# Two quads' pooled result repeated by matrix products instead of by a store and loads, with quad 0's mixing ordered sooner

## The chip, the cores and the metric

The kernel runs on one core of a Trainium2 chip. That core has a matrix engine (TensorE), a vector engine (VectorE), a scalar engine (ScalarE), a general engine (GpSimd) and a queue engine (SyncE) that here issues nearly all DMA transfers. Each of them works through its own list of instructions in order and meets the others by semaphores. TensorE's clock is granted at one of two levels, 1.2 and 2.4 GHz; the profile gives it as a share of the upper one.

The metric is the device time of one execution in microseconds, the median of several runs.

## The reference

The input is an attention problem of 4 batches, 8 heads, 576 rows and 64 columns, followed by two mixing networks. What matters here is the attention and the first step behind it:

```python
q_d = q.reshape(B, H, Sd, 4, D).mean(axis=3)        # likewise k_d, v_d: Sd = 144
out_d = sm_attn(q_d, k_d, v_d)                       # softmax attention on 144 rows
out_up = np.repeat(out_d, 4, axis=2)                 # each row four times: 576 rows
scores = where(abs(i - j) < 4, scale * q @ k.T, -1e9)
out_local = softmax(scores) @ v
x = (out_up + out_local)                             # heads side by side: 576 x 512
h = relu(x.T @ w_tok1) @ w_tok2                      # token mixing, 576 -> 256 -> 576
u = x + h.T
```

A channel network and a second mixing with sines and cosines follow. All is computed to float32 accuracy; where products run in the faster rounded format, each operand is split in a high and a low part and three products are added.

## The kernel before

Two heads make a pair (16 pairs, numbered 0 to 15), two pairs make a quad (8 quads, 0 to 7). For each pair, `pair_local` computes the banded attention of 576 rows in five blocks of 128 rows. For each quad, `quad_front` (L425) computes the pooled attention: scores `sd` on TensorE, row maxima `mxd` on VectorE, exponentials `pd` on ScalarE, transposes `pdt`, their copy `pts`, the product `od`, and the division on VectorE that gives `ods`. `ods` holds 144 pooled rows of four heads, and every row is needed four times, on four neighbouring partitions.

That repetition is done through memory (L509 to L519): `ods` is stored in two parts into `od_d` and `ot_d`, and read back into the tile `xu` by three loads whose source has a repeated axis. `add_pooled` (L595) then adds `xu` to the pair's local result `x`, and `token_mix` (L598) splits the sum into `xh` and `xl` and multiplies with the token weights `w1h` and `w1l`. Those weights come in as 64-bit floats and are converted in steps on ScalarE (L199, L201), VectorE (L203, L206, L215), GpSimd (L219), ScalarE (L221) and VectorE (L223).

Every such routine is a generator, cut by `yield` into steps. The table `ORDER` says in which sequence the steps are run, and thereby the order on every engine: no scheduler moves them in this part. `P` is the load of a pair's q and k, `W` of its values, `K` pools a pair, `F` is the quad's attention, `L` the pair's local attention, `A` adds the pooled result, `T` is the token mixing, `G` converts token weights. `F0` at its eighth place stores `ods` of quad 0, at its ninth it loads `xu`.

PSUM has eight banks in this part: four single ones, tag "mm", for `od` and the mixing's products, and two tiles of two banks, tag "big", through which all of `s`, `sd`, `pt`, `pdt` and `o` pass. So a product into a big tile waits until the last reader of the tile before the one before is done.

`warm` (L312) issues products on zeros ahead of the first pairs' scores. `low2` is a pool of tiles that the mixing of odd blocks uses later.

Of the kernel before, what the change touches and what calls it, by code (L numbers as in the profile page):

```python
# [12 lines left out]
F32 = mybir.dt.float32  # L13
# [17 lines left out]
FIRST = 1  # L31
ROWS = ((8, 9), (0, 2), (4, 6), (2, 3))
ORDER = """
G3 P0 G2 I*2 P1 G3 P4 G3 V0 P2 G3 K0 G3 G2 I G2 I L0*2 P3 K1 F0 W1 L0 F0 L1 L0 G3 F0 V0 L1*2 P5 V0 L2 W0 G2 K2 V0 G2
F0 G1 L1 V1 F0 L2 K3 G0 G6 K4 L0 F0 L0 L2 L1 G2 F1 L2 K5 L1 L0 F1 G1*2 F1 F0 V1 W3 L0 F1 G5 G0 L1 F0 G0 F1 G6 F2 L1 G0
P6 W2 G5 G6 L3 V1 F2 F0 V1 L3 G6 F2 F1 L3 G1 G4 F1 L2 P7 L5 L2 K6 L5 F1 G1 L3 A0 V2 X0 A1 L3 G1 T0 L5 G0 T0 L2 G2 F1
L3 G0 G4 F2 G5 T0*2 V2 X2 L2 G6 W5 F2 K7 V2 L4*2 E0.0*2 T0 L4 V3 V2 A2 L3 E0.1 L5 G4 L4 W4 L5 G6 L5 G4 L3 X2 F3 G5 P8
P9 A3 G4 F2 G5 E0.1 T1 G4 G5 T0 F2 V3 L4 F3 F2 T0 L4 V3 X2 F3 L6 V3 L6 X7 T0 P11 L6 X2 X0 F3 K8 U0.0 L6 T0 X2 X0 U0.0
F3 L4 U0.0 V4 K9 F2 F3 X0 L6 L4 L6 T1 F4 U0.1 X0 F3 T1 L5 U0.1 X0 T1 U0.1 F4 X7 X4 V4 F3 T1 X7 F4 W6 L5 X7 E1.1 F4
E1.0 E1.1 L8 V4 L8 X7 E1.0 X1 A4 F4 T1 P10 A5 T1 X2 T2 L8 T1 U1.0*2 T2 T1 U1.0 X1 F3 L7 X7 L7 T2 X1 T2 X4 X5 K10 X1 L8  # L40
L6 U1.1*2 L7 T2 E2.0 U1.1 W7 X4 L7 V4 X1 L7 F4 W9 L7 L6 X4 E2.1 E2.0 C0 E2.1 T2 X1 L8 K11 X5 L7 T2 X5 L8 W8 L9*2 L7 X5
P13 T2 P12 L9 L10 C0 A6 F5 X4 C0 U2.0 L10 U2.0 X5 U2.0 C0 X3 F5 X6 F4 F5 C0 A7 F4 L10 T3 X4 F5 L9 V5 T3 H0.1 L8 U2.1
F5 T2 H0.1 H0.0 K12 T3 L9 U2.1 X5 C0 L9 U2.1 K13 F4 X6*2 L10 T3 X3 W13 H0.0 X6 H0.2 F6 E3.0*2 V5 P14 T3 F6 V5 H0.2 F6
C0 V6 V5 L8 X3 E3.1 L9 H0.3 F5 E3.1 X3 W10 L9 F6 X3 F5 L10 V6 A9 T3 F5 T3 V6 U3.0 L10 K14 T3 V6 U3.0 X6 U3.0 T3 H0.3
# [42 lines left out]
PAIRS = ((0, 1), (5, 4))  # L87
LOWER, WIDE = 2, 2
MIX = 384
NMIX = 6  # L90
WARM = [24] + [12] * 3 + [0] * 12
DEEP = [4, 4]
# [4 lines left out]
DTOK = 256  # L97
DCH = 1536
NB = 5
# [15 lines left out]
def kernel(  # L115
# [16 lines left out]
    act, dve, pool, pe, sp = nc.scalar, nc.vector, nc.gpsimd, nc.tensor, nc.sync  # L132
# [13 lines left out]
    idt, diag, msk = fixed[:, 0:128], fixed[:, 128:132], fixed[:, 132:].bitcast(BF16)  # L146
# [19 lines left out]
    def converted(stage, hi, lo, parts, sub, add, gaps=repeat(1), room=None, keep=(), fine=0):  # L166
# [10 lines left out]
        else:  # L177
            both = room
            if isinstance(room, tuple):
                both = room[0].tile([128, 4, MIX], F32, tag=room[1], name=f"raw_{at}")  # L180
            both = both.rearrange("p k n -> p (k n)")
# [71 lines left out]
    low2 = tc.alloc_tile_pool(name="low2", bufs=1, side="right")  # L253
# [12 lines left out]
    def evict_hidden(ps, n, at):  # L266

        h1 = hp.tile([128, MIX], F32R, tag="h1", name=f"g1_{at}")
        h2 = hp.tile([128, MIX], F32R, tag="h2", name=f"g2_{at}")

# [10 lines left out]
    def columns(t, i):  # L281

        return t[:, i * MIX : i * MIX + MIX].rearrange("(k p) n -> p k n", p=128)

    mmp = ctx.enter_context(tc.tile_pool(name="mma", bufs=8 - 2 * WIDE, space=PSUM))

    actx = ExitStack()
    sb1 = actx.enter_context(tc.tile_pool(name="a1", bufs=1))
# [29 lines left out]
    loaded, values, pooled, xs_of, xus, hiddens, outs = {}, {}, {}, {}, {}, {}, {}  # L318

    def step(name, gen):  # L320
        gens[name] = gen

    def constants():
        sp.dma_start(fixed, consts)
        yield
        pool.memset(zero, 0.0)
        for t in pbuf:
            pool.memset(t, 0.0)
        yield
        act.copy(id16, idt)  # L330
        yield

    def tok1(kb, room):
# [91 lines left out]
    def quad_front(Q):  # L425
        b, hh = divmod(Q, 2)
        at = f"{b}_{hh}"
# [3 lines left out]
        for p in range(2):  # L431
            for c in range(4):
                for j in range(2):
# [4 lines left out]
                        start=True,  # L438
                        stop=True,
                    )  # L440
            for j in range(2):
                c = 2 * j + p
# [4 lines left out]
                    start=True,  # L447
                    stop=True,
# [4 lines left out]
            out=mx[:, 0:4].rearrange("p (j a) -> p j a", j=2),  # L453
# [4 lines left out]
        for j in range(2):  # L458
            r = slice(64 * j, 64 * j + 64)
# [11 lines left out]
        for j in range(2):  # L471
            r = slice(64 * j, 64 * j + 64)
# [6 lines left out]
        for o, i in ((128, 0), (256, 4)):  # L479
            for c in range(4):  # L480
                out = pt[32 * c : 32 * c + 32, 1, o : o + 128]
# [24 lines left out]
        ods = sb1.tile([128, 5, 64], F32, tag="ods", name=f"ods_{at}")  # L506
        dve.tensor_tensor(out=ods, in0=odv[:, :, 0:64], in1=rd.to_broadcast([128, 5, 64]), op=ALU.mult)
        yield
        base, tail = od_d[b][hh], ot_d[b][hh]  # L509
        sp.dma_start(base.rearrange("s k n -> k s n"), ods[:, 0:4, :].rearrange("p c d -> p (c d)"))  # L510
        sp.dma_start(tail.rearrange("s (c d) -> c s d", c=4), ods[:, 4, :])
        yield
        xu = sb1.tile([128, NB, DTOK], F32, tag="xu", name=f"xu_{b}_{hh}")
# [152 lines left out]
    def mix(i, p0, p1):  # L666
# [3 lines left out]
        if not p0:  # L670
            ut = (low2 if odd else b2).tile([128, 4, MIX], F32, tag="ut", name=f"ut_{at}")
            sp.dma_start(ut, columns(uT_d, i))
            mixes["ut", i, p0] = ut
        uh, ul = ((low2 if odd else b1).tile([128, 4, MIX], F32R, tag=f"u{p}", name=f"u{p}_{at}") for p in "hl")
        if p0:
# [233 lines left out]
    def mix_rest(i):  # L909
        ut = (cells["utx"] if i in [q for _, q in PAIRS] else b2).tile([128, 4, MIX], F32, tag="ut", name=f"ut_{i}_{LOWER}")  # L910
        sp.dma_start(ut, columns(xT_d, i))
        mixes["ut", i, LOWER] = ut
        yield
# [35 lines left out]
    def lazily(f):  # L949
        yield from f()  # L950
# [123 lines left out]
    def first_split():  # L1074
        cells["xhl0"], steps = split_x(0, cells["x0"][0])
        for st in steps:
            st()
            yield

    step("I", constants())  # L1080
    for n in range(4 * B):
        for name, f in (("P", load_pair), ("W", load_values), ("K", pool_pair), ("L", pair_local), ("A", add_pooled)):
            step(f"{name}{n}", f(n))
    for Q in range(2 * B):
        for name, f in (("V", pool_values), ("F", quad_front), ("T", token_mix)):
            step(f"{name}{Q}", f(Q))
        for i in range(2):
            step(f"E{Q}.{i}", token_hidden(Q, i))
            step(f"U{Q}.{i}", token_out(Q, i))
# [9 lines left out]
    for i in chain(range(4 * LOWER, 28), range(31 + FIRST, 39), range(41, 45)):  # L1099
        step(f"X{i}", lazily(lambda i=i: cells["X", i]()))  # L1100
    for i in range(NMIX):
        step(f"J{i}", mix_rest(i))
# [28 lines left out]
    with tc.manual_schedule(engines={act.engine, dve.engine, pool.engine, pe.engine, nc.sync.engine}):  # L1131
        for e in ORDER:
            name, _, times = e.partition("*")
# [7 lines left out]
    sb1 = ctx.enter_context(tc.tile_pool(name="c1p", reuse_waits="tile", bufs=1))  # L1141
# [75 lines left out]
    T0, T1 = slice(0, HALF), slice(HALF, S)  # L1217
# [119 lines left out]
    for b in range(B):  # L1337
        x, xn = xx
        uh = sb1.tile([128, 4, S], F32R, tag="uh", name=f"cuh_{b}")
        ul = sb1.tile([128, 4, S], F32R, tag="ul", name=f"cul_{b}")  # L1340
# [94 lines left out]
```

## Time and profile before

| | |
|---|---|
| Median of 3 runs | 685.61 us (683.41 to 687.0) |
| The profiled execution | 681.57 us, its span 679.8 us, mean granted clock 0.99 |
| TensorE busy | 655.9 us, 96% of the span |
| VectorE busy | 521.0 us, 77% |
| ScalarE busy | 321.2 us, 47% |
| GpSimd busy | 98.5 us, 14% |
| DMA | 109.93 MB, mean 162 GB/s |
| Chain that ended last | TensorE 84%, VectorE 8%, DMA 3%, ScalarE 3% |

The page's slices of 17 us show TensorE at 6, 7, 6 and 9 tenths at first and at 9 or more from then on. The DMA engines are at 7 to 8 tenths in the first slices. The attention part lies in the first 190 us, mixed with the first mixing products; the rows below are from it but for one. In a timeline row, the bracket at the end gives how long the engine stood still ahead of the row and what released it. "Issue" there means that nothing in the profile explains the idle time.

### The profile page before, as it was taken

How to read it: one execution, taken by the hardware profiler on the slowest of the kernel's cores; microseconds unless marked ns; L12 is line 12 of the kernel's file. 1: busy time of each engine (PE TensorE's matmuls, PEld its weight loads, DVE VectorE, ACT ScalarE, POOL GpSimd, SP SyncE). 2: the span in 40 equal slices, each digit the busy share in tenths (PEclk: the TensorE clock that was granted, in tenths of full speed). 3: DMA queues.
4: the chain of work that ended last, by engine and by line, in shares of the span. 5: the costliest groups of instructions: out<-in, count | busy, mean ns of one | idle time of the engine just before them, and what ended most of it. 6: DMA issues, size and time to landing. Idle time of an engine off the chain costs nothing.

```text
span 679.8 us, 17390 instructions
## 1 busy us (share of the span) xinstructions
PE 655.9 (96%) x7320; PEld 626.7 (92%) x7320; DVE 521.0 (77%) x952; ACT 321.2 (47%) x632; POOL 98.5 (14%) x92
## 2 busy tenths in 40 slices
PE   6769899999999999999999999999999999999997
PEld 4558789889999999999999999999999998998997
DVE  5889998697542888998988867677898748857837
ACT  4566667455341674535434523154647326527311
POOL 3223322305000333300101200012000000000000
PEclk9889999999999999999999999999999999999999
DMA  8787788757343785527263762699410330140202
GB/s 282 239 277 229 250 274 260 252 179 238 110 157 104 242 293 186 202 62 207 66 194 127 209 142 85 238 324 279 130 63 0 112 114 1 62 141 1 71 1 69
DMA packets 93022, 109.93 MB, mean 162 GB/s; under 512 B 46881, under 2 KB 69537, under 8 KB 92945
## 3 DMA queue, kind: packets, MB, share of 16 engines
q1 hardware_dynamic: 92080, 106.08, 49.6%
q0 software_dynamic: 864, 2.75, 1.0%
q8 instruction: 57, 0.93, 0.6%
q14 instruction: 21, 0.16, 0.1%
HBM read 79.13 MB, written 29.69 MB: 160 GB/s over the span
## 4 chain that ended last, share of the span: by engine, by line
PE 84%; DVE 8%; DMA 3%; ACT 3%; SPq 1%; issue 1%; DVEq 0%; ACTq 0%
PE y L157 6%; PE y L158 6%; PE y L159 6%; PE c L157 4%; PE c L158 4%; PE c L159 4%; PE c L699 4%; PE c L702 4%; PE c L700 4%; PE c_p L905 3%; PE c_p L902 3%; PE c_p L903 3%; PE t L157 2%; PE t L159 2%; PE t L158 2%; DMA qk<-qkT 2%
## 5 line engine op out<-in xcount | busy, mean ns | idle before, releaser
L157 PE MATMUL y<-wrh,zh 128*128 128x288 f32 x256 | 75.0, 296 | 0.8 <-ACT zh L151 0.8
L158 PE MATMUL y<-wrl,zh 128*128 128x288 f32 x256 | 74.9, 296 | 0.0
L159 PE MATMUL y<-wrh,zl 128*128 128x288 f32 x256 | 72.9, 295 | 0.0
L219 POOL TENSOR_TENSOR ww<-ww,raw 128x512 int32<-128x512 int32 (+2 forms) x30 | 41.1, 1373 | 159.2 <-DMA raw<-w_ch 52.5
L157 PEld LDWEIGHTS y<-wrh,zh 128*128 128x128 f32 x256 | 48.0, 188 | 1.1 <-ACT zh L151 1.1
L158 PEld LDWEIGHTS y<-wrl,zh 128*128 128x128 f32 x256 | 48.0, 188 | 0.0
L159 PEld LDWEIGHTS y<-wrh,zl 128*128 128x128 f32 x256 | 47.3, 188 | 0.0
L219 POOL TENSOR_TENSOR raw<-raw 128x512 int32<-128x512 int32 (+2 forms) x16 | 20.0, 1249 | 136.7 <-DVE raw L215 74.1
L1212 DVE TENSOR_TENSOR cx<-y,cx 128x288 f32<-128x288 f32 x32 | 14.4, 455 | 30.3 <-PE y L159 29.9
L151 ACT CAST cuh<-cx 128x288 fp32r<-128x288 f32 (+1 forms) x16 | 8.8, 553 | 57.5 <-DVE cx L1212 57.4
L157 PE MATMUL th<-thh,cxh 128*128 128x512 f32 (+1 forms) x92 | 31.6, 343 | 0.0
L158 PE MATMUL th<-thl,cxh 128*128 128x512 f32 (+1 forms) x92 | 31.6, 343 | 0.0
L159 PE MATMUL th<-thh,cxl 128*128 128x512 f32 (+1 forms) x92 | 31.6, 343 | 0.0
L199 ACT ACTIVATE ww<-raw 128x512 f32<-128x512 f32 (+2 forms) x30 | 19.5, 649 | 25.3 <-DVE c1l L223 9.4
L921 DVE SCALAR_TENSOR_TENSOR g<-c,g 128x384 fp32r<-128x384 f32 x40 | 21.1, 550 | 12.9 <-ACT g L918 12.9
L918 ACT ACTIVATE g<-c 128x384 fp32r<-128x384 f32 x40 | 19.1, 490 | 24.4 <-PE c L159 24.3
L201 ACT ACTIVATE raw<-raw 128x512 int32<-128x512 uint32 (+3 forms) x46 | 29.5, 640 | 0.0
L568 PE MATMUL o<-vw,plt 38*32 38x65 f32 x1280 | 18.0, 236 | 6.9 <-issue 3.6
L929 DVE TENSOR_TENSOR ut<-c,ut 128x384 f32<-128x384 f32 x32 | 17.1, 551 | 9.8 <-PE c L702 9.8
L568 PEld LDWEIGHTS o<-vw,plt 38*32 38x32 f32 x1280 | 15.4, 110 | 9.6 <-issue 4.8
L157 PE MATMUL t<-w2h,h 128*128 128x256 f32 (+1 forms) x64 | 21.6, 337 | 0.0
L157 PE MATMUL c<-uh,c1h 128*128 128x384 f32 x64 | 21.4, 334 | 0.0
(390 smaller groups left out, 2266.6 us busy)
## 6 DMA issues: line engine op xcount, KB each, us to landing
raw<-w_ch SPq DMA_DIRECT2D x27, 512.0 KB
qk<-qkT SPq DMA_DIRECT2D x16, 582.0 KB
xT<-ut SPq DMA_DIRECT2D x12, 768.0 KB
vd<-vtok SPq DMA_DIRECT2D x8, 650.0 KB
vw<-vloc SPq DMA_DIRECT2D x32, 146.2 KB
uT<-us SPq DMA_DIRECT2D x16, 288.0 KB
ut<-uT SPq DMA_DIRECT2D x6, 768.0 KB
ut<-xT SPq DMA_DIRECT2D x6, 768.0 KB
```

Of the source, the lines that this page charges most:

```text
L157: pe.matmul(out, lh, rh, start=start, stop=False, skip_group_check=again)
L158: pe.matmul(out, lh, rl, start=False, stop=False, skip_group_check=again)
L159: pe.matmul(out, ll, rh, start=False, stop=stop, skip_group_check=again)
L201: act.activation(f, words[:, :, 0], AF.Copy, scale=2.0**-29)
L219: pool.tensor_tensor(out=w.bitcast(I32), in0=w.bitcast(I32), in1=f, op=ALU.add)
L568: pe.matmul(o[r : r + 32, 5 * j + i // 2], pts[h : h + W, i // 2, r : r + 32], vw[h : h + W, g, :], start=True, stop=True,)
L699: pe.matmul(ps[:, 0:MIX], h[:, cb % 2, d], h1, start=cb == cbs[0], stop=False)
L700: pe.matmul(ps[:, 0:MIX], l[:, cb % 2, d], h1, start=False, stop=False)
L702: pe.matmul(ps[:, 0:MIX], weight[cb // 2][2][:, cb % 2, d], h2, start=False, stop=cb == cbs[-1])
L902: pe.matmul(ps[:, 0:MIX], h[:, cb % 2, d], h1, start=cb == cbs[0], stop=False)
L903: pe.matmul(ps[:, 0:MIX], l[:, cb % 2, d], h1, start=False, stop=False)
L921: dve.scalar_tensor_tensor(out=h2, in0=ps, scalar=0.0, in1=h1.bitcast(F32), op0=ALU.max, op1=ALU.subtract)
```

## The change

For quads 0 and 1 (`UP`), `quad_front` no longer stores and loads. Instead TensorE multiplies `ods` with a matrix of ones and zeros, `spread`, that has each row's one in four columns. Four products with 64 rows of contraction and 256 columns give the first 128 pooled rows, four with 128 rows and 64 columns the last 16. They go into three single PSUM banks (`up`), and ScalarE copies these into `xu`. The matrix is made once from the identity by four copies on ScalarE. The other six quads keep the store and loads.

The table is written anew in its first lines: the adds `A0` and `A1` stand ahead of pair 6's pooling, the first step of `T0` ahead of the copies of quad 1, and the load `W0` ahead of `P5`. Later lines hold the same steps.

```diff
-G3 P0 G2 I*2 P1 G3 P4 G3 V0 P2 G3 K0 G3 G2 I G2 I L0*2 P3 K1 F0 W1 L0 F0 L1 L0 G3 F0 V0 L1*2 P5 V0 L2 W0 G2 K2 V0 G2
+G3 P0 G2 I*2 P1 G3 P4 G3 V0 P2 G3 K0 G3 G2 I G2 I L0*2 P3 K1 F0 W1 L0 F0 L1 L0 G3 F0 V0 L1*2 W0 P5 V0 L2 G2 K2 V0 G2
...
+UP = (0, 1)
...
         act.copy(id16, idt)
+        both = low2.tile([128, 4, MIX], F32, tag="ul", name="spread").rearrange("p k n -> p (k n)")
+        spread["main"] = both[:, 0:256].rearrange("p (e n) -> p e n", e=2)
+        spread["rest"] = both[:, 256:768].rearrange("p (c n) -> p c n", c=4)
+        for h in range(2):
+            r = slice(64 * h, 64 * h + 64)
+            out = both[r, 0:256].rearrange("p (q r) -> p q r", r=4)
+            act.copy(out, idt[r, 64 * h : 64 * h + 64].unsqueeze(2).to_broadcast([64, 64, 4]))
+        rest = both[:, 256:768].rearrange("p (c j q r) -> p c j q r", c=4, j=2, r=4)
+        one = idt.rearrange("p (c q) -> p c q", c=4)[:, :, 16:32]
+        for j in range(2):
+            act.copy(rest[:, :, j], one.unsqueeze(3).to_broadcast([128, 4, 16, 4]))
         yield
...
+        if Q in UP:
+            xu = xus[Q] = sb1.tile([128, NB, DTOK], F32, tag="xu", name=f"xu_{b}_{hh}")
+            up = [mmp.tile([128, 512], F32, tag="mm", name=f"up_{at}_{h}") for h in range(3)]
+            for e in range(2):
+                for h in range(2):
+                    r = slice(64 * h, 64 * h + 64)
+                    out = up[h][:, DTOK * e : DTOK * e + DTOK]
+                    rhs = ods[r, 0:4, :].rearrange("p h d -> p (h d)")
+                    pe.matmul(out, spread["main"][r, e], rhs, start=True, stop=True)
+            for c in range(4):
+                out = up[2][:, 64 * c : 64 * c + 64]
+                pe.matmul(out, spread["rest"][:, c], ods[:, 4, :], start=True, stop=True)
+            yield
+            for h in range(2):
+                act.copy(xu[:, 2 * h : 2 * h + 2].rearrange("p b n -> p (b n)"), up[h])
+            act.copy(xu[:, 4], up[2][:, 0:DTOK])
+            yield
+            return
         base, tail = od_d[b][hh], ot_d[b][hh]
         sp.dma_start(base.rearrange("s k n -> k s n"), ods[:, 0:4, :].rearrange("p c d -> p (c d)"))
```

What the change moves is seen best in the order of the instructions. In these rows tiles carry batch and place in it, then a serial number: `od_0` and `xu_0` belong to quad 0, `pts_1` to quad 1, `mxd_0_728` and `pd_0_780` to quad 2, which is quad 0 of batch 1. Lines are those of each version.

TensorE at the place of the first new products, before (`o_1` is pair 1's local product):

```order
L477 MATMUL pdt_1_602<-fixed,pd_1_579 128x128 x5
L482 MATMUL pdt_1_602<-fixed,pd_1_579 32x128 x8
L568 MATMUL o_1_620<-vw_1_266,plt_1_525 32x65 x40
L434 MATMUL sd_0_672<-qkd_0_448 32x144 x8
L443 MATMUL sd_0_672<-qkd_0_448 32x144 x2
```

and with the change:

```order
L491 MATMUL pdt_1_607<-fixed,pd_1_584 128x128 x5
L496 MATMUL pdt_1_607<-fixed,pd_1_584 32x128 x8
L600 MATMUL o_1_625<-vw_1_271,plt_1_530 32x65 x40
L531 MATMUL up_0_0_667<-ods_0_594,spread 128x256
L531 MATMUL up_0_1_668<-ods_0_594,spread 128x256
L531 MATMUL up_0_0_667<-ods_0_594,spread 128x256
L531 MATMUL up_0_1_668<-ods_0_594,spread 128x256
L534 MATMUL up_0_2_669<-ods_0_594,spread 128x64 x4
L448 MATMUL sd_0_690<-qkd_0_453 32x144 x8
```

Eight products stand between pair 1's local product and quad 2's scores. Quad 1's eight follow pair 5's scores in the same way.

ScalarE at the same place, before (`raw_446` and `ww_669` are the third token weight in conversion):

```order
L199 ACTIVATE raw_444<-raw_444 128x512
L201 ACTIVATE raw_444<-raw_444 128x512
L485 COPY pts_1_666<-pdt_1_602 128x512
L486 COPY pts_1_666<-pdt_1_602 128x384
L199 ACTIVATE ww_669<-raw_446 128x288
L201 ACTIVATE raw_446<-raw_446 128x288
```

and with the change, where the same weight is `raw_451` and `ww_687`:

```order
L200 ACTIVATE raw_449<-raw_449 128x512
L202 ACTIVATE raw_449<-raw_449 128x512
L537 COPY xu_0_666<-up_0_0_667 128x512
L537 COPY xu_0_666<-up_0_1_668 128x512
L538 COPY xu_0_666<-up_0_2_669 128x256
L499 COPY pts_1_684<-pdt_1_607 128x512
L500 COPY pts_1_684<-pdt_1_607 128x384
L200 ACTIVATE ww_687<-raw_451 128x288
```

Three copies that read `up` stand ahead of quad 1's `pts` and of that weight.

ScalarE some ten rows on, before (`plt_2` is pair 2's transposed weights, `pbuf_120` pair 3's exponentials, `xh_0` quad 0's first mixing operand):

```order
L562 COPY plt_2_838<-pt_2_827 128x128
L221 CAST w1h<-raw_393 128x512
L553 ACTIVATE pbuf_120<-pbuf_120 128x10x38
L603 CAST xh_0_902<-x_0_600 128x1280
L221 CAST w1h<-raw_444 128x512
```

and with the change:

```order
L594 COPY plt_2_854<-pt_2_843 128x128
L585 ACTIVATE pbuf_120<-pbuf_120 128x10x38
L635 CAST xh_0_858<-x_0_605 128x1280
L537 COPY xu_1_904<-up_1_0_905 128x512
L537 COPY xu_1_904<-up_1_1_906 128x512
L538 COPY xu_1_904<-up_1_2_907 128x256
L222 CAST w1h<-raw_398 128x512
L222 CAST w1h<-raw_449 128x512
```

The first cast to `w1h` has moved from before `pbuf_120` to behind `xh_0` and the three copies of quad 1. VectorE's matching subtraction `w1l` keeps its place ahead of pair 5's row maxima.

## Rows read from the trace of the kernel before

**Rows 1.** Windows of 4 us: length, busy us (and instructions) per engine, granted clock, DMA share

```profile
20.00:24.00 4.00, 3.89 (x121) 3.04 (x122) 2.95 (x7) 1.93 (x5) 0.00 (x0) 1.00 1.02 340
24.00:28.00 4.00, 1.56 (x74) 1.28 (x77) 3.84 (x8) 3.88 (x11) 1.41 (x1) 1.00 0.46 169
28.00:32.00 4.00, 2.91 (x128) 2.49 (x131) 3.53 (x11) 2.21 (x5) 0.57 (x1) 0.53 0.59 169
...
48.00:52.00 4.00, 4.00 (x31) 3.25 (x30) 3.86 (x7) 2.27 (x6) 2.35 (x3) 0.50 0.88 280
```

**Rows 2.** A window of 10 us, same columns

```profile
80.00:90.00 10.00, 10.00 (x298) 9.27 (x297) 9.66 (x15) 7.57 (x16) 2.84 (x3) 1.00 0.86 282
```

**Rows 3.** TensorE waits from 200 us on: total us, times, longest

```profile
PE y L157 <- ACT zh L151: 0.8, 1, 0.8
```

**Rows 4.** Chain of waits, 34 to 46 us: start, us, what

```profile
35.44 6.58 DMA xu<-ot
```

**Rows 5.** Timeline of TensorE: start, us, operation, idle before and releaser

```profile
20.58 0.65 PE L493 MATMUL od<-vl,pts 128*32 128x260 f32 x8
21.04 0.64 PE L496 MATMUL od<-vs,pts 128*32 128x65 f32 x32
...
29.87 1.54 PE L568 MATMUL o<-vw,plt 38*32 38x65 f32 x79 [1.09 <-issue]
...
45.51 1.49 PE L568 MATMUL o<-vw,plt 38*32 38x65 f32 x80 [3.27 <-DVE pbuf L546]
47.36 1.33 PE L477 MATMUL pdt<-fixed,pd 128*128 128x128 f32 x5 [0.36 <-ACT plt L562]
...
52.51 0.34 PE L530 MATMUL s<-fixed,id 128*128 128x190 bf16 x2
```

**Rows 6.** Timeline of ScalarE

```profile
12.11 0.52 ACT L553 ACTIVATE pbuf<-pbuf 128x380 f32<-128x380 f32 x1 [4.52 <-DVE pbuf L546]
...
26.44 0.76 ACT L473 ACTIVATE pd<-sd,mxd 64x144 f32<-64x144 f32 x2
...
28.83 0.59 ACT L485 COPY pts<-pdt 128x512 f32<-128x512 f32 x1 [0.33 <-PE pdt L482]
...
29.69 0.48 ACT L199 ACTIVATE ww<-raw 128x288 f32<-128x288 f32 x1
...
38.95 0.59 ACT L561 COPY plt<-pt 128x512 f32<-128x512 f32 x1 [0.85 <-PE pt L558]
...
39.73 0.62 ACT L221 CAST w1h<-raw 128x512 fp32r<-128x512 f32 x1
...
43.74 1.26 ACT L603 CAST xh<-x 128x1280 fp32r<-128x1280 f32 x1 [2.97 <-DVE x L595]
```

**Rows 7.** Timeline of VectorE

```profile
25.95 1.71 DVE L215 SCALAR_TENSOR_TENSOR raw<-raw 128x512 uint32<-128x512 uint32 x1
...
30.60 0.69 DVE L215 SCALAR_TENSOR_TENSOR raw<-raw 128x512 uint32<-128x512 uint32 x1
...
32.72 0.88 DVE L203 TENSOR_SCALAR ww<-ww 128x288 f32<-128x288 f32 x1
...
34.71 0.75 DVE L452 TENSOR_REDUCE mxd<-sd 128x4 f32<-128x576 f32 x1
...
42.15 1.56 DVE L595 TENSOR_TENSOR x<-x,xu 128x640 f32<-128x640 f32 x2 [1.94 <-DMA xu<-ot]
43.62 0.68 DVE L223 TENSOR_TENSOR w1l<-raw,w1h 128x512 fp32r<-128x512 f32 x1
...
47.71 1.33 DVE L206 TENSOR_SCALAR ww<-ww 128x288 uint32<-128x288 uint32 x1
...
53.12 0.43 DVE L643 SCALAR_TENSOR_TENSOR h<-t,h 128x256 fp32r<-128x256 f32 x1 [0.75 <-ACT h L640]
53.73 0.55 DVE L545 TENSOR_REDUCE mx<-s 128x10 f32<-128x380 f32 x1 [0.17 <-PE s L533]
```

**Rows 8.** Timeline of GpSimd

```profile
25.70 1.41 POOL L398 TENSOR_TENSOR vd<-vd 128x650 f32<-128x650 f32 x1 [9.37 <-DMA vd<-vtok]
```

More of the change, by code (lines that the diff above doesn't have):

```diff
@@ L33 @@
 ORDER = """
-G3 P0 G2 I*2 P1 G3 P4 G3 V0 P2 G3 K0 G3 G2 I G2 I L0*2 P3 K1 F0 W1 L0 F0 L1 L0 G3 F0 V0 L1*2 P5 V0 L2 W0 G2 K2 V0 G2
[L35 to L41, printed above, removed]
+G3 P0 G2 I*2 P1 G3 P4 G3 V0 P2 G3 K0 G3 G2 I G2 I L0*2 P3 K1 F0 W1 L0 F0 L1 L0 G3 F0 V0 L1*2 W0 P5 V0 L2 G2 K2 V0 G2
+F0 G1 L1 V1 F0 L2 K3 G0 G6 K4 L0 F0 L0 L2 L1 G2 F1 L2 K5 L1 L0 F1 G1*2 F1 F0 V1 W3 L0 F1 G5 G0 L1 F0*2 G0 F1 G6 F2 L1
+G0 P6 W2 G5 G6 L3 V1 F2 V1 L3 G6 F2 F1 L3 G1 G4 F1 A0 A1 L2 P7 L5 L2 L3 T0 K6 L5 F1*2 G1 V2 X0 L3 G1 L5 T0 G0 L2 G2 L3
+G0 G4 F2 G5 T0*2 V2 X2 L2 G6 W5 F2 K7 V2 L4*2 E0.0*2 T0 L4 V3 V2 A2 L3 E0.1 L5 G4 L4 W4 L5 G6 L5 G4 L3 X2 F3 G5 P8 P9
+A3 G4 F2 G5 E0.1 T1 G4 G5 T0 F2 V3 L4 F3 F2 T0 L4 V3 X2 F3 L6 V3 L6 X7 T0 P11 L6 X2 X0 F3 K8 U0.0 L6 T0 X2 X0 U0.0 F3
+L4 U0.0 V4 K9 F2 F3 X0 L6 L4 L6 T1 F4 U0.1 X0 F3 T1 L5 U0.1 X0 T1 U0.1 F4 X7 X4 V4 F3 T1 X7 F4 W6 L5 X7 E1.1 F4 E1.0
+E1.1 L8 V4 L8 X7 E1.0 X1 A4 F4 T1 P10 A5 T1 X2 T2 L8 T1 U1.0*2 T2 T1 U1.0 X1 F3 L7 X7 L7 T2 X1 T2 X4 X5 K10 X1 L8 L6
+U1.1*2 L7 T2 E2.0 U1.1 W7 X4 L7 V4 X1 L7 F4 W9 L7 L6 X4 E2.1 E2.0 C0 E2.1 T2 X1 L8 K11 X5 L7 T2 X5 L8 W8 L9*2 L7 X5
 P13 T2 P12 L9 L10 C0 A6 F5 X4 C0 U2.0 L10 U2.0 X5 U2.0 C0 X3 F5 X6 F4 F5 C0 A7 F4 L10 T3 X4 F5 L9 V5 T3 H0.1 L8 U2.1
@@ L321, in step @@
         gens[name] = gen
+    spread = {}
     def constants():
```

## The prediction

> **What bounds the kernel now.** I read the windows first. From 80 us on TensorE is busy 10.00 of 10 us, with VectorE at 9.66 [rows 2], and after 200 us TensorE waits for another engine once, for 0.8 us [rows 3]. So the end is TensorE's, and an edit made in the first 55 us pays exactly what it moves TensorE at about 80 us. In the first 52 us TensorE is not full: 1.56 of 4 us in 24 to 28, and its granted clock is 0.53 in 28 to 32 and 0.50 in 48 to 52, that is on its lower level, 1.2 GHz, nearly or all of that time [rows 1].
>
> The chain of waits says why. The load of quad 0's repeated result has its last part issued by 35.44 us and lands 6.58 us later [rows 4], and the two adds that use it start at 42.15 on VectorE, after 1.94 us of standing still [rows 7]. Behind the adds stand w1l and the row maxima of pair 5. TensorE's next product, o_2 at 45.51, waited 3.27 us for the end of those maxima and their differences [rows 5]; after that gap pdt_2 and the first mixing product run from 47.36 to 52.51 at the lower level [rows 5, 1]. I call these steps by their tiles: up_0 and up_1 are the new products, xu_0 and xu_1 their copies on ScalarE, ww_451 the third token weight that is converted.
>
> **What goes, at no gain of its own.** For two quads eight DMA issues leave SyncE, with 0.8 MB of traffic for each quad by the tiles' shapes. Later loads are issued sooner. Pair 0's values also pass the load of pair 5's q and k. If that fills TensorE's hole before 26 us, the next thing late is pdt_1: it needs the last exponentials of quad 1, which start at 26.44 and take 0.76 us [rows 6]. So the hole is worth nothing. The four copies that make the ones and zeros, each below 0.5 us by the 512-column copy of 0.59, lie in ScalarE's 4.52 us of idle time before 12.11 [rows 6]; without that cover they would cost 1.6 us.
>
> **The cost of up_0.** The trace has no plain f32 product of this shape. The nearest is the group of four 260-column products on 32 columns each, which takes 0.46 us from 20.58 to 21.04 [rows 5]. If these four run side by side, one takes 0.46 us; if one after the other, 0.115. So the four 256-column products of up_0 take 0.46 to 1.84 us, and its four 64-column ones a quarter of that: 0.6 to 2.3 us together at the upper clock, 1.2 to 4.6 at the lower one. I take the case in which the two halves of the rows go as a pair and the last four singly: 0.92 + 0.46 = 1.4 us, and 2.8 at the lower level, because o_1, right ahead of it, took 1.54 us at a granted 0.53 [rows 5, 1].
>
> The Trainium skill (TensorEngine Tiling (Array Packing), section Tiling Modes) says that row tiles of 64 by 128 work in parallel, but that a change of tiling mode drains the array. That is the pair I took, plus two drains that no row here prices; a sum without pairs would be 2.3 us at full clock and lie at my upper bound.
>
> **The chain after the change, step by step.** The stall on the load goes, but the order puts new waits into ScalarE's line: xu_0's three copies stand in front of pts_1 and ww_451, and xu_1's three in front of w1h. ScalarE works in order, so what is queued behind them waits with them.
>
> 1. o_1 runs 29.87 to 31.4 as before; up_0 ends 2.8 later, at 34.2.
> 2. ScalarE does the first two copies while up_0's last products run. The third takes 0.4 us, by 0.59 for 512 columns; then pts_1, 0.86 (28.83 to 29.69), and ww_451's first operation, 0.48 [rows 6]. That ends at 35.95 where it ended at 30.2.
> 3. VectorE, which took ww_451 at 32.72 [rows 7], now waits for it until 35.95: a new wait of 3.2 us, longer than the 1.9 removed. Its three operations took 1.99 us (to 34.71). At the 0.69 us that the slowest of them needs for 512 columns at 30.60, 288 columns need at most 3 x 0.39 = 1.2; so 1.2 to 2.0, and I take 1.2: 37.1.
> 4. From quad 2's maxima (VectorE, 34.71) over its exponentials on ScalarE and pt_2 on TensorE to plt_2 on ScalarE (38.95) took 4.2 us [rows 6, 7]: 41.3. plt_2, 0.8 (to 39.73): 42.1. Exponentials of pair 3, 0.5: 42.6. xh, 1.26: 43.8. In between A0 and A1 are done: they took 1.5 us, from 42.15 to 43.62 [rows 7], the load no longer holds them, and the work ahead of them is late by up_0's 2.8 us at most. I estimate that they come sooner by about a microsecond; their result then waits in ScalarE's line.
> 5. xu_1, three copies like xu_0's, 1.4: 45.2. w1h, 0.5 of its 0.62 before the next can start: 45.7. VectorE's w1l, the maxima and the differences that free the buffer took 1.9 us, from 43.62 to o_2's start at 45.51: o_2 starts at 47.6. That is 2.1 us late [rows 5 to 7].
>
> Then part of it is given back. ScalarE has a second w1h, three small casts and plt_3 to do, 2.6 us after 45.7, so pdt_2 starts at 48.3, 1.0 late. From pdt_2 to the end of the first mixing product took 5.15 us at the lower clock [rows 5]: 53.5 if it is low again, 50.9 if not. On VectorE the way from w1l at 43.62 to the maxima of pair 4 at 53.73 took 10.1 us, of which 0.75 was a wait for ScalarE and 0.9 is what the operation at 47.71 took (1.33) over its 0.39 [rows 7]; with these back, 45.7 + 8.5 = 54.2, 0.5 late. With the low clock the maxima wait for TensorE and start 1.0 late. TensorE's gap ahead of o_2 stays about 3 us long, as it was, but VectorE has work to catch up: I take +0.7 us, between the two, and -0.5 to +2.0 with the spread of up_0 and o_1. From there both engines are full, and nothing gives it back.
>
> **Sum.** The span of 679.8 becomes 680.5, the profiled execution's 681.57 becomes 682.3. The median of the runs shown is 685.61, 4.04 above that execution; with 0.7 it is 686.3, and that is my number.
>
> **Rivals.**
> *The stall goes and nothing takes its place.* For it: up_0 may run at the upper clock, and VectorE's 1.71 us operation at 25.95 (0.69 at 30.60 for the same shape) lay beside a GpSimd add at 25.70 [rows 7, 8] that now gets its data sooner. If that operation shrinks, o_1 starts 1.0 sooner; if up_0 takes 1.4, step 2 ends 2.4 sooner, VectorE's new wait is under 1 us, o_2 starts at about 45.2, and the clock stays up through the mixing. VectorE then gains the 1.9 us of the old stall at least, and by the 3.4 us that steps 1 and 2 win against my chain, less the 0.7, 2.7: 682.9 to 683.7, with 683.3 the middle, and up to 3.5 if the conversion at 47.71 shrinks too. Against it: the DMA engines are full in 20 to 24 (1.02) [rows 1], so that add hardly moves, and both conditions must hold. The Trainium skill (SBUF — State Buffer, section SBUF: two separate sides) has VectorE and GpSimd share a port under an exclusive lock, so that the loser waits a whole operation; by that rule the 1.0 us comes back whole or stays whole. The trace agrees with the wait, 1.71 against 0.69.
> *Slower: ScalarE's line behind up_0.* One mechanism: up_0 takes its upper bound, 4.6 us at the lower clock. Then every step from 2 on is 1.8 later, VectorE's new wait is 5 us, o_2 starts at 49.4, and TensorE stands still for some 4 us ahead of it, so that the mixing runs low too: 0.7 + 1.8 + 1.0 = 3.5, 689.1. It decides from the point where ww_451's first operation on ScalarE ends after 37.5 us.
> *The change does not do what it says:* the load was hidden by other work, and the new order only swaps equal waits: 685.6. The row maxima that o_2 waited for speak against it.
>
> **How the numbers follow.** What a measurement here can tell from no change is about 0.5%, 3.4 us. My forecast with its own range of 685.1 to 687.6 has 0.50, the equal swap 0.10, the faster rival 0.23, the slower one 0.17. The runs before spread over 3.6 us, so of either rival about half ends beyond 0.5% once the slower one's own spread is counted, and little of the rest: faster 0.12, same 0.75, slower 0.13. The range takes in both rivals but for their ends: 682.5 to 689.3.
>
> **What would show it.** Right: VectorE idle for 2 us or more at ww_451 with ScalarE as releaser; ScalarE's xu_0 copies right after up_0; o_2 after 46.5; another idle piece on VectorE at w1l, released by w1h. Wrong: up_0 done in under 2 us with the clock up by 32, o_2 before 45.5, the mixing at full clock. Then the time is near 683.3. Also wrong: TensorE at 80 us shifted by something that comes after 54 us, which I hold to be unchanged.

## The result, and the profile after

The changed kernel takes 689.78 us (median of 22 runs, 682.65 to 692.17) and the kernel before, on the same chip, 684.05 (22 runs, 680.23 to 687.26): a ratio of 1.0069 (95% interval 1.0047 to 1.0091). It is slower, by 4.7 us going by the ratio; the medians lie 5.7 us apart. The profiled execution of the changed kernel took 682.65 us, the shortest of its 22, so its rows show the mechanism at its best and not the usual loss. Of the twelve experiments below, nine have profiles within 2 us of their medians; the exceptions are named.

The first 58 us of that execution went better than before. TensorE's timeline (start, length, operation, what it stood idle for before it):

```profile
29.85 1.14 PE L600 MATMUL o<-vw,plt 38*32 38x65 f32 x80
30.92 1.14 PE L531 MATMUL up<-ods,spread 64*128 64x256 f32 x8
31.99 1.10 PE L534 MATMUL up<-ods,spread 128*128 128x64 f32 x8
33.02 0.48 PE L448 MATMUL sd<-qkd 64*32 64x144 f32 x16
...
46.19 1.28 PE L600 MATMUL o<-vw,plt 38*32 38x65 f32 x80 [2.46 <-DVE pbuf L578]
47.40 1.33 PE L491 MATMUL pdt<-fixed,pd 128*128 128x128 f32 x5
...
51.69 0.34 PE L562 MATMUL s<-fixed,id 128*128 128x190 bf16 x2
...
57.29 0.48 PE L448 MATMUL sd<-qkd 64*32 64x144 f32 x16 [0.84 <-ACT plt L594]
```

up_0 lasts from 30.92 to 33.02, o_2 starts at 46.19 instead of 45.51, but the first mixing product ends at 51.69 instead of 52.51 [rows 5]. VectorE's rows:

```profile
34.76 0.31 DVE L204 TENSOR_SCALAR ww<-ww 128x288 f32<-128x288 f32 x1 [2.30 <-ACT ww L200]
...
39.37 1.55 DVE L627 TENSOR_TENSOR x<-x,xu 128x640 f32<-128x640 f32 x2
...
44.32 0.69 DVE L224 TENSOR_TENSOR w1l<-raw,w1h 128x512 fp32r<-128x512 f32 x1 [2.23 <-ACT w1h L222]
```

The adds stand at 39.37 without a wait, where they began at 42.15 after 1.94 us [rows 7]. In its place VectorE stands still twice for ScalarE, 2.30 us at ww_451 and 2.23 us at w1l. ScalarE's rows show what it did meanwhile:

```profile
32.09 1.07 ACT L537 COPY xu<-up 128x512 f32<-128x512 f32 x2 [3.52 <-PE up L531]
33.13 0.37 ACT L538 COPY xu<-up 128x256 f32<-128x256 f32 x1
33.40 0.59 ACT L499 COPY pts<-pdt 128x512 f32<-128x512 f32 x1
...
34.25 0.48 ACT L200 ACTIVATE ww<-raw 128x288 f32<-128x288 f32 x1
...
42.43 1.07 ACT L537 COPY xu<-up 128x512 f32<-128x512 f32 x2
43.38 0.39 ACT L538 COPY xu<-up 128x256 f32<-128x256 f32 x1
43.65 1.16 ACT L222 CAST w1h<-raw 128x512 fp32r<-128x512 f32 x2
```

xu_0's copies stand ahead of pts_1 and ww_451, xu_1's ahead of w1h, as forecast. The granted clock was 0.78 in 28 to 32 and 0.72 in 48 to 52, against 0.53 and 0.50 [rows 1]. Windows (length, busy us of TensorE, weight loads, VectorE, ScalarE, GpSimd, clock, DMA share, GB/s):

```profile
28.00:32.00 4.00, 4.00 (x110) 2.75 (x108) 3.76 (x11) 0.57 (x2) 0.59 (x1) 0.78 0.63 182
48.00:52.00 4.00, 4.00 (x44) 3.06 (x46) 3.86 (x8) 2.15 (x6) 1.35 (x2) 0.72 0.57 158
```

Up to here it is a gain. It is lost behind 57 us. Between 68 and 76 us TensorE has two holes that the profile puts down to "issue", that is to nothing it shows (I call such an idle piece a hole):

```profile
70.68 0.32 PE L514 MATMUL od<-vs,pts 128*32 128x65 f32 x7 [1.01 <-issue]
...
75.41 0.31 PE L600 MATMUL o<-vw,plt 38*32 38x65 f32 x5 [1.80 <-issue]
```

The second one lies inside a local product o, five product records before its end, where no wait is written. From 80 us on TensorE is as full as it was [rows 2].

A measure for what follows: the kernels share two waits on TensorE, one at sd_3, some 58 us in, and the one for zh at 481 us [rows 3]. From sd_3 on TensorE runs the same number of records in both. Before, and then after (the zh row; its sd_3 stands above):

```profile
58.05 0.48 PE L434 MATMUL sd<-qkd 64*32 64x144 f32 x16 [0.84 <-ACT plt L562]
...
481.38 0.41 PE L157 MATMUL y<-wrh,zh 128*128 128x288 f32 x1 [0.84 <-ACT zh L151]
```

```profile
482.36 0.40 PE L158 MATMUL y<-wrh,zh 128*128 128x288 f32 x1 [1.19 <-ACT zh L152]
```

So it is 481.38 - 58.05 = 423.3 us before and 482.36 - 57.29 = 425.1 after, even in the shortest execution.

### The profile page after: what moved, and what is told of

Its sections match the earlier page's. It is cut to its first block, busy times and chain, and to the rows that moved or that the text cites. A ratio compares the mean times of both kernels' runs of the same rounds, so it can differ in the third digit from the quotient of the medians.

```text
span 680.9 us, 17450 instructions
## 1 busy us (share of the span) xinstructions
PE 659.2 (97%) x7352; PEld 629.3 (92%) x7352; DVE 519.3 (76%) x952; ACT 324.7 (48%) x642; POOL 100.0 (15%) x92
## 4 chain that ended last, share of the span: by engine, by line
PE 83%; DMA 6%; DVE 5%; ACT 2%; issue 2%; SPq 1%; DVEq 0%
PE y L158 6%; PE y L159 6%; PE y L160 6%; PE c L731 4%; PE c L159 4%; PE c L158 4%; PE c L734 4%; PE c L732 4%; PE c L160 4%; PE t L158 2%; PE t L159 2%; DMA wrl<-wr_l 2%; PE t L160 2%; PE o L600 2%; PE th L159 2%
## 5 line engine op out<-in xcount | busy, mean ns | idle before, releaser
L950 ACT ACTIVATE g<-c 128x384 fp32r<-128x384 f32 x40 | 19.2, 490 | 26.5 <-PE c L160 26.4
```

The lines of the kernel that those rows point to most:

```text
L950: act.activation(h1, ps, AF.Relu)
```

## Experiments: undoing the parts

These four ran together; the kernel before took 684.17 us beside them (29 runs). Theory A is that of the prediction: new waits in ScalarE's line set the loss. Theory B: the granted clock sets it.

**The change again.** No edit.

> The changed kernel as it is, once more, for a second profile and the granted clock of each execution. Its first profile was of its fastest execution (682.65 us, mean clock 0.995) of 22; over those 22 the time falls by 4.9 us for each 0.01 of mean clock. Theory A (ScalarE's line): the new waits on VectorE, 2.3 us at ww_451 and 2.2 us at w1h in that profile, are what costs; the second profile shows the same two waits, longer if the median is to be explained, and no more time at the lower clock than before's two stretches of 6.8 us. Theory B (the clock): the waits are as in the first profile, but the mean clock is about 0.985, so TensorE is at 1.2 GHz for about 20 us, and the time about 690.

Measured: 689.93 us (12 runs), ratio 1.0075 (1.0042 to 1.0108). The loss is there again. Its profile, of an execution of 684.37 us (5.6 us below the median), has the two holes (at 70.90 and 75.35), and VectorE's two waits are 2.45 and 2.22 us, about as long as in the first profile. The median of the granted clock is 0.988 over these 12 runs and 0.985 over the 29 of the kernel before: the change's loss is there without a lower clock, against theory B.

**The products alone.** The new products in the order of before.

```
-ORDER = """ G3 P0 ... L1*2 W0 P5 V0 L2 G2 K2 ...   (the changed table)
+ORDER = """ G3 P0 ... L1*2 P5 V0 L2 W0 G2 K2 ...   (the table of before)
```

> The products and copies of the change with the table of the kernel before, so that ScalarE copies xu_0 behind pts_1 and ww_451, and casts w1h before xh. Theory A: without these two waits it is no slower than before, ratio to before 0.995 to 1.000 (the adds start 1 to 2 us sooner). Theory B: the products fill TensorE's idle time, and what the clock does is set by where its idle time lies; with o_2 still behind VectorE's line the clock falls as before, ratio 1.000 to 1.004.

Measured: 693.53 us (6 runs), ratio 1.0151 (1.0115 to 1.0186), the slowest of the four, where theory A expected no loss or a gain and theory B 1.004 at most. Its TensorE rows and windows at 80 us:

```profile
80.59 0.43 PE L600 MATMUL o<-vw,plt 38*32 38x65 f32 x5 [3.27 <-issue]
```

```profile
76.00:80.00 4.00, 1.32 (x98) 1.16 (x85) 3.92 (x8) 2.28 (x5) 1.34 (x1) 0.95 0.54 205
80.00:84.00 4.00, 3.41 (x19) 3.23 (x19) 2.88 (x7) 2.18 (x8) 2.00 (x2) 0.50 0.75 218
84.00:88.00 4.00, 4.00 (x37) 3.66 (x36) 0.57 (x2) 0.96 (x3) 0.01 (x1) 0.69 0.64 180
```

The same place of the same product, 3.27 us of hole, and the granted clock on its lower level right behind it, where the kernel before has 1.00 [rows 2]. That is a step which neither theory had. Here the clock has a part too: its median over the runs is 0.980.

**The order alone.** The kernel before with the changed table of order; no new products.

```
-ORDER = """ (the table of before)
+ORDER = """ (the changed table)
```

> The table of the change with the store and loads of the kernel before. The adds A0 and A1 now stand ahead of pair 6's pooling on VectorE and wait for the load (about 42 us), and w1h is behind xh on ScalarE. Theory A: VectorE stands still 1.2 us longer ahead of the adds and about 1 us at w1l; ratio to before 1.002 to 1.005. Theory B: as TensorE's gap ahead of o_2 grows by 2 us, more time at the lower clock; ratio 1.005 to 1.010, mean clock below before's by 0.003 or more.

Measured: 686.19 us (12 runs), ratio 1.0040 (1.0014 to 1.0065). That lies in theory A's range of 1.002 to 1.005. But its profile has a hole of 2.14 us at 59.57, in the products of sd_3 itself, again called issue, and none inside that o.

**ScalarE's line mended.** The changed kernel with xu_0's copies behind the token weights (F0 further back) and w1h ahead of xu_1's copies (G1 further forward).

```
-... L0 F0*2 G0 F1 G6 F2 L1 G0 P6 W2 G5 G6 L3 V1 ... L2 L3 T0 K6 L5 F1*2 G1 V2
+... L0 F0 G0 F1 G6 F2 L1 G0 P6 W2 G5 G6 F0 L3 V1 ... L2 L3 G1 T0 K6 L5 F1*2 V2
```

> The change with two moves in the table: ScalarE copies xu_0 behind pts_1 and the two weights instead of ahead, and casts the first w1h ahead of xh and xu_1's copies. Theory A: both new waits on VectorE go (2.3 and 2.2 us become under 0.3 each), o_2 starts at 43 to 44.5 us instead of 46.2, and the time is 2 to 4 us below the change's, at before's or up to 0.5% below it. Theory B: the gap ahead of o_2 shrinks below 1 us, so the clock holds through the mixing; then it gains 4 us or more against the change and its mean clock is above 0.990; if instead the clock stays at 0.985, the time stays within 2 us of the change's although the waits are gone.

Measured: 687.68 us (12 runs), ratio 1.0056 (1.0029 to 1.0083). It was 2.25 us below the change run beside it, but the intervals overlap. Both waits of VectorE are gone from its profile, o_2 starts at 44.56, and it is still slower than the kernel before: theory A says where the waits are; it does not say where most of the loss is. The profile has the hole at 77.70, of 2.72 us:

```profile
77.70 0.43 PE L600 MATMUL o<-vw,plt 38*32 38x65 f32 x5 [2.72 <-issue]
```

## What the holes have in common

Counted from the start of the trace over all records of TensorE and its sequencer, the holes stand at fixed numbers (I count from 1; the expectations below count from 0, so that their 193 and 3521 are 194 and 3522 here). The hole inside the o is ahead of record 3522 in the change, in the run of it again, in products_alone and in line_mended; that of 26.4 us ahead of record 962. In all 14 profiles of this case TensorE has 71 idle pieces of 0.5 us or more that are called issue behind 14 us, and 68 of them stand ahead of record 194 plus a multiple of 256; the other three stand ahead of the first record of o_1. Of the 68, those behind the 700th record end 2.2 to 2.8 us after the start of a packet of the instruction queue, and the 256 records ahead of each had been run in 2.1 to 5.9 us. In the longest one, of 4.23 us (below), TensorE stops at 115.50, the packet starts at 117.11 and the work goes on at 119.73. A whole trace has 57 to 59 such packets, one in 12 us: 57 in the kernel before, with 14,744 records, and 59 in the run with the most, 15,065. The DMA queues' rows (packets, MB, share of time), of before and of the changed kernel:

```profile
q8 instruction: 57, 0.93, 0.6%
```

```profile
q8 instruction: 58, 0.95, 0.6%
```

A packet has 16,384 bytes. I read this as TensorE's instructions coming in blocks of 256, and a hole where short products use one up before the next has landed. The new products bring 64 records more, 32 for each quad, and so one packet more. The work slides over the blocks' borders by 64 records.

The Trainium skill (Runtime: NRT & Kernel Launch, section Instruction fetch mechanics) says that instructions are refilled in blocks of 16 KiB, 256 instructions, by the sequencer's own DMA queue while the current block runs, and that the cost of crossing a border is mostly hidden. The trace agrees with the 256. It agrees with the last only for most crossings: of the 57 or so of an execution, 2 to 8 show a hole of 0.5 us or more, but these cost up to 4.23 us each.

Theory C: the loss is made by the place of these holes. Theory D: by the products' time and the waits, wherever the holes lie. To tell them apart I moved the borders without touching the change: small dummy products (32 columns of weights, 16 columns moved) at the very start, where TensorE waits for its first operands. 112 of them last 3.15 us:

```profile
1.21 3.15 PE L561 MATMUL s<-zero 128*32 128x16 bf16 x112 [1.21 <-POOL zero L329]
4.30 2.31 PE L316 MATMUL s<-zero 128*128 128x320 bf16 x8
9.01 0.50 PE L564 MATMUL s<-fixed,id 128*128 128x190 bf16 x2 [2.39 <-ACT id L333]
```

## Experiments: moving the borders

Each product makes two records, a weight load and a product. The edit, with two counts; none of it feeds the result:

```
-WARM = [24] + [12] * 3 + [0] * 12
+WARM = [BIG] + [12] * 3 + [0] * 12
...
+        for _ in range(SMALL if n == 0 else 0):
+            pe.matmul(s[0:32, 0, 192:208], zero[:, 0:32], zero[:, 0:16], start=True, stop=True)
         warm(s[:, 0, 192:512], WARM[n])
```

Before with 64 more and the change with 128, 192 and 256 more ran beside a kernel before of 685.05 us (29 runs), the products alone and the mended line with 192 more beside 685.66 (23), before with 256 more and quad 0 alone beside 685.44 (23).

**The kernel before, 64 more** (32 small, 24 big).

> The kernel before, with 32 small dummy products added behind the 24 ahead of pair 0's scores: 64 records more for TensorE, as many as the new products have, and nothing else changed. Theory C: record 3521 now falls where it falls in the change, a hole of 1 us or more inside an o at 75 to 80 us, and the time is 686.5 to 690 us, a ratio of 1.004 to 1.009. Theory D: the small products lie in time in which TensorE waits for its first operands, so 683.5 to 685 us, a ratio of 0.999 to 1.001.

Measured: 690.52 us (12 runs), ratio 1.0083 (1.0055 to 1.0110). Nothing but 32 dummy products, and the whole loss of the change is there (0.5 us above theory C's range in us, inside that of the ratio). Its profile took 690.43 us. TensorE's rows, then its windows:

```profile
60.55 0.48 PE L434 MATMUL sd<-qkd 64*32 64x144 f32 x16 [0.84 <-ACT plt L564]
...
78.63 0.43 PE L570 MATMUL o<-vw,plt 38*32 38x65 f32 x5 [2.45 <-issue]
...
154.94 0.34 PE L570 MATMUL o<-vw,plt 38*32 38x65 f32 x12 [1.01 <-issue]
176.02 0.28 PE L620 MATMUL t<-xs,w1s 128*128 128x256 f32 x1 [0.77 <-issue]
201.20 0.28 PE L158 MATMUL t<-xl,w1h 128*128 128x256 f32 x1 [0.62 <-issue]
490.24 0.40 PE L157 MATMUL y<-wrh,zh 128*128 128x288 f32 x1 [0.85 <-ACT zh L151]
```

```profile
76.00:80.00 4.00, 1.55 (x24) 1.23 (x12) 3.89 (x8) 3.16 (x10) 1.08 (x1) 0.80 0.68 194
80.00:84.00 4.00, 4.00 (x29) 4.00 (x29) 1.69 (x4) 1.06 (x5) 2.01 (x2) 0.77 0.86 264
```

From sd_3 to zh it takes 429.7 us, 6.4 more than before. Four holes give 2.45 + 1.01 + 0.77 + 0.62 = 4.9, where the kernel before has one of 0.82 in this stretch (at 101.38). The lower clock gives at most 4 x (0.20 + 0.23) = 1.7. Together that is 5.8 of the 6.4.

**The kernel before, 256 more** (140 small, 12 big): the borders fall as in before.

> The kernel before with 12 dummy products of the old size and 140 small ones in the place of the 24: 256 records more, so that the holes fall at the places of the work at which they fell before. Theory C: no hole over 1 us inside an o at 75 to 80 us, 683.5 to 686.5 us, a ratio of 0.998 to 1.003, well below the 690.5 of the kernel before with 64 more. If the small products themselves were what made that one slower, this one, with four times as many, is at 690 us or above.

Measured: 682.51 us (12 runs), ratio 0.9967 (0.9940 to 0.9995). So the small products do no harm; four times as many, and the loss is gone. It is the fastest version of the study, 1 us below the range that theory C gave.

**The change, 192 more** (112 small, 8 big): with its own 64 that is 256.

> The change, with the 24 dummy products ahead of pair 0's scores made into 8 of the old size and 112 small ones (32 columns of weights, 16 columns moved), so that TensorE has 192 records more at the start, while its operands are still loaded. Theory C (place of the holes): in all traces so far TensorE's holes that the profile calls issue stand ahead of record 193 plus a multiple of 256, counted over its weight loads and products; the new products bring 64 records, so the holes fall at another place of the work, one of them (record 3521) into a local product o at 75 to 80 us, where nothing covers it, and the granted clock falls after it. With 192 more the records stand as in the kernel before: no hole over 0.5 us inside that o, and 682 to 686.5 us, that is a ratio to before of 0.997 to 1.003. Theory D (the products' own time and the waits that they bring into ScalarE's and VectorE's lines): the place doesn't matter, 688 to 691.5 us, as the change by itself.

Measured: 687.51 us (12 runs), ratio 1.0026 (0.9994 to 1.0058), a little above the range that theory C gave in us and inside that of the ratio. The hole inside the o is gone; from sd_3 (63.20) to zh (487.49) it takes 424.3 us. In this profile most of what is left lies ahead of sd_3: the clock is on its lower level for 20.5 us there, against 13.6 in the kernel before.

**The change, 256 more** (144 small, 8 big): the borders as in the change.

> The change, with 8 dummy products of the old size and 144 small ones in the place of the 24, so that TensorE has 256 records more at the start. Theory C: the places come round again to those of the change, the hole inside the o at 75 to 80 us is there (1.5 us or more) and the time is 688 to 692 us. Theory D: the same time as with 192 more, 688 to 691.5 us. If instead the small products themselves do something (to the clock or to the first scores), both this kernel and the one with 192 more move alike against the change.

Measured: 688.64 us (12 runs), ratio 1.0068 (1.0033 to 1.0104), with the hole back and 426.8 us between the two waits:

```profile
77.97 0.31 PE L602 MATMUL o<-vw,plt 38*32 38x65 f32 x5 [2.45 <-issue]
```

The granted clock stays at 1.00 behind this hole; behind the one of the same length in before with 64 more it fell. So a hole does not always bring the lower clock with it.

**The change, 128 more** (80 small, 8 big).

> The change, with 8 dummy products of the old size and 80 small ones in the place of the 24: 128 records more. Theory C: the holes fall 128 records sooner in the work than in the change, so the one of 75 to 80 us leaves the end of that o; where the next long one falls I can't say beforehand, and the time may lie anywhere from 683 to 692 us, but differ from that with 192 and that with 256 more by over 1.5 us from at least one. Theory D: within 1 us of both.

Measured: 703.75 us (6 runs), ratio 1.0254 (1.0205 to 1.0303), by far the slowest, and far above the 692 us that theory C gave as its upper end. TensorE's rows and the window of the longest hole:

```profile
84.91 1.31 PE L602 MATMUL o<-vw,plt 38*32 38x65 f32 x69 [2.35 <-issue]
...
119.73 0.59 PE L567 MATMUL s<-qk 64*32 64x38 f32 x35 [4.23 <-issue]
...
186.39 0.71 PE L567 MATMUL s<-qk 64*32 64x38 f32 x39 [1.86 <-issue]
```

```profile
116.00:120.00 4.00, 0.27 (x33) 0.27 (x33) 3.01 (x8) 2.45 (x8) 0.00 (x0) 0.74 0.97 367
120.00:124.00 4.00, 4.00 (x45) 3.92 (x27) 3.11 (x4) 1.25 (x2) 0.00 (x0) 0.50 0.80 276
```

Behind sd_3 the long holes now lie inside an o and inside two pairs' scores. Theory D, which had this within 1 us of the two others, is refuted: 15 us apart.

**The products alone, 192 more** (108 small, 12 big, the order of before).

> The new products in the order of before (the kernel of products_alone, 693.5 us), with TensorE's 192 records more at the start (12 dummy products of the old size and 108 small ones in the place of the 24). Theory C: the hole of 3.27 us inside the o at 80 us goes, and with it the lower granted clock behind it; the time falls by 5 to 9 us, to 684.5 to 688.5 us, a ratio of 1.000 to 1.006. If the order of before were itself bad for the products (their results come while nothing on VectorE asks for them yet), the place of the records would not mend it: 691 us or more.

Measured: 687.79 us (12 runs), ratio 1.0025 (0.9995 to 1.0055). That is in theory C's range. Of the 1.51% of products_alone 1.26 are gone by the borders alone. Its profile, of its shortest execution (681.30 us), takes 423.3 us between the waits (57.76 and 481.01), as before.

**ScalarE's line mended, 192 more** (108 small, 12 big).

> The change with ScalarE's line put right (the kernel of line_mended, 687.7 us), with 192 records more for TensorE at the start. Theory C: no hole inside the o at 77 us, 683 to 686 us, a ratio of 0.997 to 1.002; it is 1 to 3 us below the change with 192 more, as line_mended was 2.3 below the change. If the order of ScalarE's line counts for nothing, 687 to 688 us, as the change with 192 more.

Measured: 686.90 us (12 runs), ratio 1.0031 (0.9999 to 1.0063): no hole inside the o, but 0.9 us above theory C's range, and the same as the two others with 192 more. With the borders in place the order of ScalarE's line counts for nothing that can be seen.

**The products for quad 0 alone, 224 more** (`UP = (0,)`, the order of line_mended, 126 small, 10 big).

> A version that might beat both: the order of line_mended, the new products for quad 0 alone (quad 1's result again goes out and comes back by DMA, which nothing on VectorE waited for), and 224 records more, which with the 32 of the one set of products makes 256. Theory C: no hole inside the o at 75 to 80 us; against line_192_more (686.9 us) 2.1 us of products less on TensorE and three copies less on ScalarE ahead of w1h: 683 to 686.5 us. If quad 1's load now comes later than its adds, these wait on VectorE and it is 687 us or more.

Measured: 686.76 us (12 runs), ratio 1.0026 (0.9990 to 1.0062). It beats neither, and lies 0.3 us above theory C's range. In its profile the o is clear, but the block's border next to it, ahead of record 3522, which with 256 more in all lies in the products of an sd, shows 1.80 us at 76.49; products_192_more has 0.70 at the same place. With 2.31 us at 108.35 and five smaller ones its holes behind sd_3 come to 6.9 us. The borders say where a hole can open; how long it is differs from one execution to the next.

The two waits and the ratios together. The third column adds up the holes between the two waits, from 0.15 us on, the fourth takes half of the time there that the clock was on its lower level:

| kernel | sd_3 to zh, us | holes, us | lower clock, us | ratio to before |
|---|---|---|---|---|
| before | 423.3 | 0.8 | 0 | 1 |
| before, 256 more | 423.3 | 0.6 | 0 | 0.9967 |
| products alone, 192 more | 423.3 | 1.0 | 0 | 1.0025 |
| change, 192 more | 424.3 | 0.5 | 0 | 1.0026 |
| line mended, 192 more | 424.9 | 0.6 | 0 | 1.0031 |
| change | 425.1 | 4.1 | 0 | 1.0069 |
| change again | 426.3 | 4.5 | 0 | 1.0075 |
| change, 256 more | 426.8 | 4.3 | 0 | 1.0068 |
| line mended | 429.6 | 5.2 | 1.7 | 1.0056 |
| order alone | 429.7 | 2.1 | 3.4 | 1.0040 |
| before, 64 more | 429.7 | 5.2 | 1.7 | 1.0083 |
| products alone | 430.5 | 5.6 | 3.4 | 1.0151 |
| quad 0 alone, 224 more | 431.0 | 6.9 | 1.7 | 1.0026 |
| change, 128 more | 437.9 | 11.0 | 8.5 | 1.0254 |

Without the holes and the lower clock, the stretch lies between 420.9 and 424.3 us in every row but the last (418.4): these two make nearly all of the difference, and what the products and waits add behind sd_3 is small beside them.

The three columns of times are of one execution each, the ratios are of all; quad 0 alone shows how far these can lie apart, its profile being the longest of its 12 executions (690.57 us).

## Why the prediction was right or wrong

**The number: too low.** I forecast +0.7 us, between -0.5 and +2.0, and measured +4.7. The 689.78 us lie above the upper end that took in the rivals, 689.3, and a slower kernel had a chance of 0.13.

**What bounds the kernel: right.** TensorE is full from 80 us on, and what moves it there moves the end.

**The load's stall goes and ScalarE's line puts two waits in its place: right in place, too long in size.** 2.30 us at ww_451 against 3.2; w1l at 44.32 against 45.7; o_2 at 46.19 against 47.6; pdt_2 at 47.40 against 48.3. Ten DMA issues left SyncE, not eight, since each quad had two stores and three loads.

**up_0: mis-sized both ways.** I took 1.4 us at the upper clock and 2.8 at the lower. It took 2.1, 1.07 for the four of 256 columns and 1.03 for the four of 64, which I had at a quarter of the others; up_1's two groups begin 1.06 us apart too, in a window of clock 1.00 (40 to 44). The sum without pairs, 2.3, was the nearer one. That the clock was up made this shorter than my 2.8, and with it all that hangs on it.

**The hole before 26 us would perhaps fill: it stays,** 2.55 us before and after, since it is a hole at a border (record 962) and no load fills it. VectorE's long operation beside the GpSimd add stayed too (1.73 us, the add at 25.75), as I had argued against the faster rival.

**The sum of the first 58 us: +0.7 forecast, -0.8 measured in this execution** (57.29 against 58.05), by less low clock. That is not the usual execution: most of the other profiles with the products reach sd_3 between 58.9 and 63.2 us, after a longer stay on the lower clock. Of what the early part costs on the median, only bounds are shown: with the borders of before, the three versions with the products lie at 1.0025 to 1.0031 of before, their intervals from 0.9994 to 1.0063. My +0.7 us is 1.0010 and lies inside them. Against the kernel before with 256 more, which has dummies much like theirs, they are some 0.6% behind, though not in the same set of runs. So the products and their waits probably do cost something; whether by their own time or by the clock in the first 60 us isn't settled.

**The step that failed: "TensorE at 80 us shifted by something that comes after 54 us, which I hold to be unchanged."** The instructions there are unchanged, their numbers are not. 64 records more set the borders of the blocks into other products. That alone makes the kernel before 0.83% slower, and setting the borders back takes 0.4% from the change (1.0068 to 1.0026, intervals overlapping) and 1.26% from the products alone (intervals apart). None of my rivals had it; the one on the slower side, ScalarE's line behind a long up_0, gave a time near the measured one (689.1), but that is luck: its mechanism did not happen, since ww_451's first operation ended at 34.7, not after 37.5.

What stays open: what makes a block's packet start late in the single case, and so which border shows a hole and how long it is (order_alone has its own at 59.57, with two records more than before), and why 256 more records made the kernel before 0.3% faster.

## What to carry to other kernels

Where an engine that bounds the end runs many short instructions (here TensorE; no other engine was tried), count its instructions ahead of the bound stretch as part of an edit: any that are added or taken move the borders of 256 for all that follows. Before an edit of some 0.5% is judged, try it with a few dummy instructions at the start, in idle time, that set the borders back; otherwise the place is measured and not the edit. A hole called issue that stands inside a run of like products is the sign.

## What was not expected of the hardware

Holes of up to 4.23 us inside runs of short products, with no wait written there, 68 of 71 ahead of a 256th record; 32 dummy products in idle time at the start that cost 5.5 us at the end. And a plain f32 product on all 128 rows took as long for 64 columns as one on 64 rows for 256: four of each, 1.03 and 1.07 us.
